# Attention and gated MLP on one core: other slots for the output projection's loads, four output tiles moved behind the last visit, other places for scores

## The chip, the cores and the metric

The kernel runs on one core of one Trainium2 chip. The metric is device time in microseconds (us) of one execution. Before the change three executions took 1666.72 to 1669.98 us, with a median of 1668.14 us. A separate, profiled execution took 1665.91 us; its profile spans 1664.1 us from the first to the last instruction.

## The reference

The input x is 2048 rows of 512 floats. All three parts of the result read its normalised rows.

```python
xn = _layernorm(x)
qkv = xn @ wqkv                      # 32 heads of 16
p = softmax(q k^T * 16**-0.5)        # 2048 x 2048 for each head
s = (p v, heads side by side) @ wo
r = relu(xn @ w1 + b1)               # 1792 wide
g = silu((r * r) @ w2 + b2)
out = x + s * g
```

## The kernel before, in words

**Precision.** Every product that must be exact to float32 is made of three matmuls on a high and a low part (high·high, high·low, low·high). A term list of such a product over four blocks of 128 rows has twelve matmuls.

**The loop.** After a lead (layer norm, q, k, v, written to DRAM), the attention runs in 512 *steps*. A *unit* is four heads times 512 queries; there are 32 units of 16 steps, and a step takes one block of 128 keys. For each step the kernel makes four scores on TensorE (`exp_mm`, L1255), four exponentials on ScalarE (L1261, into a `pt` tile), and four products with v (`pv_mm`, L375, called by `pv_step` two steps later). The maxima that the softmax subtracts are made a unit ahead by a second set of score matmuls (L300) and a reduction on VectorE (L308). The queue `SP` issues nearly all transfers, in program order.

**Lanes and visits.** A score has only 64 rows of contraction, so TensorE runs two at a time, one on array rows 0 to 63 and one on rows 64 to 127 (two *lanes*). The dense work (first the MLP, then the output projection) is cut into the same two lanes and mixed in by hand: `long_slots` handles four steps and one block of dense matmuls, a *visit* in two halves. At the end of a half stand the products with v of two earlier steps. When no maxima are left (`wide`), a half places ten pairs in a fixed order, a string in which `s` is a pair of scores and `D` a pair of dense matmuls. Places are counted from 0 here. In that stage the scores use five PSUM banks in turn, so a score can start only when the exponential five scores before it has been read.

**The output projection.** `wo_part` (L719) makes 14 visits from step 456 to step 511: the four tiles of output chunk 2, two of chunk 3, then the eight of chunks 0 and 1. Visit k starts at step 456 + 4k. Chunks 2 and 3 lack the last units, whose share is added later by `unit_out` (L844) with a small weight tile `w7`: for unit 30 four tiles of chunk 2 (`unit_inner`), for unit 31 the four tiles of chunk 3 (`unit_final`, after the last step). `wo_load(c)` brings the attention output of chunk c (three transfers of 512 KB, L685, for chunk 3 with a clearing on GpSimd first, L682; `wo_load_last` a fourth, L693), `wo_ask(k)` brings the gate g and, where needed, the rows of x for output tile k (L708, L713), and `wo_small` the small weight (cleared on GpSimd, L667, then loaded, `w7r`, L670). `fill` is a list of 24 matmuls for two tiles of chunk 3, kept to cover waits behind the last visit (L800).

**Due times.** `later(n, fn)` puts fn off: `begin(st)` at the start of each step runs what has come due, in the order in which it was put on the list. A call put off while such a list is being run can run at the next step at the earliest. The evacuation of a finished unit is a chain of such calls: the sums are taken out by a small transfer (`evac_sums`, L393), inverted on VectorE (`evac_recip`, L399), written and read back (L402, L407), multiplied in on GpSimd (L413 to L415) and stored (L422). VectorE works in program order, so a late sum holds everything behind the reciprocal.

Of the kernel before, what the change touches and what calls it, by code (L numbers as in the profile page):

```python
# [16 lines left out]
P = 128  # L17
S = 2048
D = 512
# [21 lines left out]
def kernel(  # L41
# [54 lines left out]
    with ExitStack() as ph:  # L96
# [84 lines left out]
        def later(n, fn):  # L181
            waiting.append((now[0] + n, fn))
# [470 lines left out]
            wos["w"] = wot  # L653

        def wo_pools():
            wos["f"] = right(wstk, "fp", 6)
            wos["oc"] = right(wstk, "ocp", 3)
            tail["p"] = right(wstk, "tailp", 1)
            free_pt.extend(
                tail["p"].tile([P, 512], F32, name=f"pt{NPT + i}") for i in range(4)  # L660
            )

        def wo_small():

            tp = tail["p"]
            raw = tp.tile([P, D], F32, name="w7r")
            nc.gpsimd.memset(raw, 0.0)  # L667
            for j in range(4):
                r = (H - 4 + j) * DH
                nc.sync.dma_start(raw[32 * j : 32 * j + DH, :], wo[r : r + DH, :])  # L670
            w7 = tail["w7"] = tp.tile([P, 2, D], F32R, name="w7")
            later(2, lambda: split((w7[:, 0], w7[:, 1]), raw))
            sel = tail["sel"] = tp.tile([P, 4], F32, name="sel")
            nc.gpsimd.tensor_scalar(
                sel, ident.rearrange("p (j r) -> p j r", r=32)[:, :, DH],
                1.0, 0.0, op0=ALU.mult, op1=ALU.add,
            )

        def wo_load(c):
            oc = wos["oc"].tile([P, 2, KO, 512], F32R, name="oc")  # L680
            if c == 3:
                nc.gpsimd.memset(oc[64:, :, 3].bitcast(F32), 0.0)  # L682
            for a, b in ((0, P), (P, 512)) if c == 2 else ((0, 512),):
                for ko in range(3):
                    nc.sync.dma_start(  # L685
                        oc[:, :, ko, a:b].bitcast(F32),
                        on_d[ko][:, :, c * 512 + a : c * 512 + b].rearrange("k p t -> p k t"),
                    )
            wos["oc", c] = oc

        def wo_load_last(c):
            n = P if c < 2 else 64
# [26 lines left out]
        def wo_part():  # L719
            for k in range(14):  # L720
                c, tt = WO_ORDER[k]
                if k == 0:
                    later(8, lambda: wo_load(3))
                    later(12, lambda: wo_load_last(3))
                if k == 4:
                    wo_load(0)
                if k == 6:
                    later(1, lambda: wo_load(1))
                if k == 5:
                    wo_load_last(0)  # L730
                if k == 9:
                    wo_load_last(1)
                if k < 12:
                    wo_ask(k + 2)
                if k == 11:
                    later(2, lambda: [wo_ask(14), wo_ask(15)])
                oc, wot = wos["oc", c], wos["w"]
                t0 = c * 512 + tt * P
                ts_ = slice(tt * P, (tt + 1) * P)
                g, xr = wos.pop(k)  # L740
                wide = c < 2 and m_free()
                if wide and "w" not in free_ps:
                    free_ps["w"] = [pm.tile([P, 512], F32, name="pm_t") for _ in range(3)]
                ps = [pd.tile([P, D], F32, name="pd_t")]
                ps.append(free_ps["w"][2] if wide else ps[0])
                if c > 1:
                    s = tail[c, tt] = tail["p"].tile([P, D], F32, name=f"ts{c}{tt}")

                def post():
                    if c > 1:  # L750
                        nc.scalar.activation(s, ps[0], AF.Copy)
                        nc.gpsimd.tensor_tensor(s, s, g, op=ALU.mult)
                        nc.gpsimd.tensor_tensor(s, s, xr, op=ALU.add)
                        return
                    if wide:
                        h = wos["f"].tile([P, D], F32, name="h", bufs=2)
                        nc.vector.tensor_tensor(h, ps[1], g, op=ALU.mult)
                        nc.gpsimd.tensor_tensor(xr, xr, h, op=ALU.add)
                    nc.vector.tensor_tensor(g, ps[0], g, op=ALU.mult)
                    nc.gpsimd.tensor_tensor(g, g, xr, op=ALU.add)  # L760
                    later(2, lambda g=g, t0=t0: nc.sync.dma_start(of[t0 : t0 + P, :], g))

                def emit(lane, n, i, m, kos):
                    r = slice(64 * lane, 64 * lane + 64)
                    a, b = ((0, 0), (0, 1), (1, 0))[i]
                    inst = nc.tensor.matmul(  # L766
                        ps[lane], oc[r, a, n, ts_], wot[r, b, n],
                        start=m == 0 and (lane == 0 or wide), stop=m == kos and (lane == 1 or wide),
                        skip_group_check=True,
                    )  # L770
                    if m == 0 and last_use[0] is not None and not wide:
                        tc.add_manual_dep(
                            inst.ins, last_use[0].ins.name,
                            mybir.DependencyInfo(
                                mybir.DependencyClass.Sync, mybir.DependencyReason.DATA
                            ),
                            reason="the other row tile is done with the bank",
                        )

                units = []  # L780
                for lane in range(2):
                    kos = [0, 1, 2] + [3] * (c < 2 or lane == 0)
                    terms = [(n, i) for n in kos for i in range(3)]
                    units.append([
                        lambda lane=lane, n=n, i=i, m=m, e=len(terms) - 1: emit(lane, n, i, m, e)
                        for m, (n, i) in enumerate(terms)
                    ])
                yield (units, post, 4) + ((True,) if wide else ())
# [55 lines left out]
        def unit_out(ps, c, tt, add, begun=False):  # L844
            hl, w7 = tail["hl"], tail["w7"]
            ts_ = slice(tt * P, (tt + 1) * P)
            for n, (i, k) in enumerate(((0, 0), (0, 1), (1, 0))):
                nc.tensor.matmul(
                    ps, hl[:, i, ts_], w7[:, k], start=(n == 0 and not begun), stop=(n == 2),
                    skip_group_check=begun,  # L850
                )
            k = 14 + 4 * (c - 2) + tt
            g, s = wos.pop(k)
            t0 = c * 512 + tt * P
            if k < 18:
                wo_ask(k + 2)
            if k == 17:
                later(1, lambda: [wo_ask(20), wo_ask(21)])
            nc.vector.tensor_tensor(g, ps, g, op=ALU.mult)
            add.tensor_tensor(g, g, s, op=ALU.add)  # L860
            if c == 2:
                later(1, lambda: nc.sync.dma_start(of[t0 : t0 + P, :], g))
            else:
                nc.sync.dma_start(of[t0 : t0 + P, :], g)

        def unit_inner(po):

            u = NU - 2
            ev = {"ot": sp.tile([P, 512], F32, name="ot", bufs=1)}
            nc.vector.tensor_scalar(ev["ot"], po, 1.0, 0.0, op0=ALU.mult, op1=ALU.add)  # L870
            for n, fn in zip(EVAC_LAST, (evac_sums, evac_recip, evac_keep, evac_back, evac_norm)):
                later(n, lambda fn=fn: fn(u, ev))

            def out(tt):
                tail["hl"] = ev["hl"]
                unit_out(pe.tile([P, 512], F32, name="se"), 2, tt, nc.gpsimd)

            for tt in range(4):
                later(9 + tt, lambda tt=tt: out(tt))

        def unit_final(po):
            ot = tail["ot"] = tail["p"].tile([P, 512], F32, name="tot")
# [2 lines left out]
            run_fill(2)  # L885
            unit_sums(pe, "se")
            run_fill(4)
            unit_norm(pe, "se", (nc.vector, nc.gpsimd))
            run_fill(len(fill))
            tail["ps", 0] = free_ps["w"][2]  # L890
            tail["ps", 1] = pd.tile([P, 512], F32, name="pd_t")
            for n, tt in enumerate((2, 3, 0, 1)):
                unit_out(
                    tail["ps", tt], 3, tt, nc.vector if n % 2 else nc.gpsimd, tt > 1
                )
# [438 lines left out]
        def long_slots(st0, units, post, wide=False):  # L1334
# [26 lines left out]
            for h in range(2):  # L1361
# [2 lines left out]
                    begin(st)  # L1364
                n = len(units[h])
                if wide:
                    for i, o in enumerate("sDDsDDsDsD"):
                        for lane in range(2):
                            if o == "s":
                                s(lane)  # L1370
# [87 lines left out]
        run_waiting(True)  # L1458
        assert not waiting and next(dn, None) is None
        fill_mms()  # L1460
        run_fill(13)
        for st_ in (NU * 16 - 2, NU * 16 - 1):
            pv_step(st_, pts.pop(st_))
        wstk.close()
# [26 lines left out]
```

## Time and profile before

| what | value |
|---|---|
| median of three executions | 1668.14 us |
| profiled execution | 1665.91 us |
| its span | 1664.1 us |
| TensorE (PE) busy | 1633.2 us, 98% |
| VectorE (DVE) busy | 1341.3 us, 81% |
| ScalarE (ACT) busy | 1185.3 us, 71% |
| GpSimd (POOL) busy | 511.2 us, 31% |
| mean granted TensorE clock | 0.998 |

PE is the matmul row and PEld the weight loads that overlap it. The times of a timeline row are its start and its length; a bracket at its end tells how long the engine sat idle before it and what ended that. `SPq` rows are issues of transfers. In the chain, each row is a piece of the work that ended last, with its start and its share.

### The profile page before, as it was taken

What the parts mean: (1) busy time and instruction counts of PE and PEld (TensorE: products, weight loads), DVE (VectorE), ACT (ScalarE), POOL (GpSimd) and SP (SyncE); (2) the same over time, 40 slices, a digit from 0 to 9 for tenths busy, and PEclk for the clock granted to TensorE, in tenths of its full rate; (3) what the DMA queues carried; (4) which work ended last, traced back from release to release, by engine and by line L of the source; (5) the groups of instructions that cost most, each with busy time, mean ns of one, the idle gap of its engine ahead of it and who ended that gap; (6) DMA issues with size and microseconds to landing.
All of it is one profiled execution on the core that took longest, in us unless ns stands there. A gap on an engine that the chain in (4) does not pass through costs nothing.

```text
span 1664.1 us, 35934 instructions
## 1 busy us (share of the span) xinstructions
PE 1633.2 (98%) x13674; PEld 981.0 (59%) x13674; DVE 1341.3 (81%) x2299; ACT 1185.3 (71%) x2344; POOL 511.2 (31%) x534
## 2 busy tenths in 40 slices
PE   6999999999999999999999999999999999999998
PEld 4898666556656665665565456555654565544454
DVE  6499888887887788877888888888888888888822
ACT  6221487778878887887787777777777777777783
POOL 4435567513312221231133113201321233113134
PEclk9999999999999999999999999999999999999999
DMA  8677555425332522352243324342332442135433
GB/s 283 164 229 252 176 172 163 128 70 162 90 93 80 155 75 80 100 139 73 78 122 106 84 71 140 93 106 80 114 95 73 106 133 64 47 115 165 136 101 123
DMA packets 152980, 201.22 MB, mean 121 GB/s; under 512 B 50856, under 2 KB 70824, under 8 KB 151272
## 3 DMA queue, kind: packets, MB, share of 16 engines
q1 hardware_dynamic: 152808, 198.93, 41.3%
q8 instruction: 108, 1.77, 0.4%
q14 instruction: 64, 0.52, 0.1%
HBM read 144.58 MB, written 53.99 MB: 119 GB/s over the span
## 4 chain that ended last, share of the span: by engine, by line
PE 93%; DVE 3%; DMA 2%; issue 1%; ACT 1%; POOL 0%; SPq 0%; DVEq 0%; POOLq 0%; ACTq 0%
PE po L375 29%; PE pd_t L234 16%; PE pm_t L300 16%; PE se L1255 15%; PE pd_t L202 6%; PE se L1013 3%; PE pd_t L766 2%; DVE mx L308 2%; PE se L964 2%; PE pd_t L1013 1%; PE po L1013 1%; DMA xc<-xn_d 1%; DMA sm<-ot 1%; PE pm_t L336 1%; DMA xt<-in_A_x_dram 0%
## 5 line engine op out<-in xcount | busy, mean ns | idle before, releaser
L308 DVE TENSOR_REDUCE mx<-pm_t 128x1 f32<-128x512 f32 x2048 | 1266.1, 683 | 224.8 <-PE pm_t L300 130.4
L1261 ACT ACTIVATE pt<-se 128x512 f32<-128x512 f32 x1750 | 926.7, 615 | 234.7 <-PE se L1255 150.2
L300 PE MATMUL pm_t<-ka,qm 64*128 64x512 f32 x2048 | 779.7, 416 | 6.1 <-DVE mx L308 5.2
L1255 PE MATMUL se<-qe,ka 64*128 64x512 f32 x2016 | 746.5, 416 | 0.0
L375 PE MATMUL po<-pt,v 128*32 128x512 f32 x3564 | 525.5, 603 | 0.0
L300 PEld LDWEIGHTS pm_t<-ka,qm 64*128 64x128 f32 x2048 | 359.2, 184 | 215.4 <-DVE mx L308 203.4
L1255 PEld LDWEIGHTS se<-qe,ka 64*128 64x128 f32 x2016 | 353.2, 184 | 113.9 <-ACT pt L1261 68.4
L234 PEld LDWEIGHTS pd_t<-xc,w1s 64*128 64x128 f32 x2352 | 295.8, 187 | 44.1 <-issue 41.9
L234 PE MATMUL pd_t<-xc,w1s 64*128 64x256 f32 x2352 | 320.5, 286 | 0.0
L234 PE MATMUL pd_t<-w2t,hT 64*128 64x512 f32 x936 | 252.6, 406 | 0.0
L375 PE MATMUL po<-ex,v 128*32 128x512 f32 x532 | 213.3, 602 | 0.0
L1261 ACT ACTIVATE ex<-se 128x512 f32<-128x512 f32 x266 | 159.4, 615 | 45.0 <-PE se L1255 22.8
L234 PEld LDWEIGHTS pd_t<-w2t,hT 64*128 64x128 f32 x936 | 160.3, 184 | 43.9 <-issue 35.2
L375 PEld LDWEIGHTS po<-pt,v 128*32 128x32 f32 x3564 | 89.4, 108 | 156.4 <-issue 139.2
L549 POOL TENSOR_TENSOR r<-r 128x512 f32<-128x512 f32 x49 | 50.9, 1040 | 316.6 <-ACT r L546 316.6
L413 POOL TENSOR_TENSOR ot<-ot,hl 128x512 f32<-128x512 f32 x31 | 39.8, 1283 | 230.0 <-DMA hl<-r_d 158.2
L568 POOL TENSOR_TENSOR u<-u,b_t 128x512 f32<-128x512 f32 x16 | 20.5, 1284 | 285.1 <-ACT u L567 229.0
L202 PE MATMUL pd_t<-w2t,hT 64*128 64x512 f32 x408 | 106.2, 392 | 0.9 <-POOL w2t L81 0.8
L202 PEld LDWEIGHTS pd_t<-w2t,hT 64*128 64x128 f32 x408 | 72.6, 184 | 10.6 <-POOL w2t L81 1.2
L766 PE MATMUL pd_t<-wot,oc 64*128 64x512 f32 x258 | 75.8, 410 | 0.0
L81 POOL TENSOR_TENSOR hT<-r,hT 128x512 fp32r<-128x512 f32 x56 | 72.3, 1291 | 4.7
L1013 PE MATMUL se<-xT,wr_t 64*128 64x512 f32 x312 | 66.2, 391 | 0.0
(132 smaller groups left out, 1206.4 us busy)
## 6 DMA issues: line engine op xcount, KB each, us to landing
w1s<-w_d SPq DMA_DIRECT2D x196, 256.0 KB
qm<-q_d SPq DMA_DIRECT2D x384, 32.0 KB
qe<-q_d SPq DMA_DIRECT2D x384, 32.0 KB
ka<-k_d SPq DMA_DIRECT2D x96, 128.0 KB
xn_d<-xT SPq DMA_DIRECT2D x8, 1024.0 KB
k_d<-hl SPq DMA_DIRECT2D x32, 256.0 KB
q_d<-hl SPq DMA_DIRECT2D x32, 256.0 KB
xc<-xn_d SPq DMA_DIRECT2D x16, 512.0 KB
```

Of the source, the lines that this page charges most:

```text
L81: (lo or nc.gpsimd).tensor_tensor(dst[1], raw, dst[0].bitcast(F32), op=ALU.subtract)
L202: mm = nc.tensor.matmul(out_, lh(r), rh(r), start=first_ and lane == 0, stop=last_ and lane == 1, skip_group_check=True,)
L234: mm = nc.tensor.matmul(out_, lh(r), rh(r), start=first_ and lane == 0, stop=last_ and lane == 1, skip_group_check=True,)
L300: nc.tensor.matmul(ps, qms[u][p][64 * j : 64 * j + 64, qb * P : (qb + 1) * P], kas[qd, p][64 * j : 64 * j + 64, kc * 512 : (kc + 1) * 512] ...
L308: return nc.vector.tensor_reduce(mxs[u][:, c, kc : kc + 1], ps, axis=AX.X, op=ALU.max)
L375: nc.tensor.matmul(po[32 * j : 32 * j + 32, :], vs[qd][:, (4 * kb + j) * VW : (4 * kb + j) * VW + 32], pts[j], start=(kb == 0), stop=(kb = ...
L413: nc.gpsimd.tensor_tensor(ot, ot, hl[:, 1].bitcast(F32), op=ALU.mult)
L549: nc.gpsimd.tensor_tensor(r, r, r, op=ALU.mult)
L766: inst = nc.tensor.matmul(ps[lane], oc[r, a, n, ts_], wot[r, b, n], start=m == 0 and (lane == 0 or wide), stop=m == kos and (lane == 1 or ...
L1013: inst = nc.tensor.matmul(out_, lh(r), rh(r), start=first_ and lane == 0, stop=last_ and lane == 1, skip_group_check=True,)
L1255: nc.tensor.matmul(se, kas[qd, j // 2][b : b + 64, kb * P : (kb + 1) * P], qes[u][j // 2][b : b + 64, :], start=True, stop=True,)
L1261: return nc.scalar.activation(pts[j], se, AF.Exp, scale=0.25)
```

## The change

The loads of the output projection are given other due times. `wo_load(3)` runs two steps after visit 0 begins instead of eight, and its three transfers are put off by 0, 1 and 2 steps (the first two come to the next step, 459, the third to 460). `wo_load(0)` and `wo_load(1)` move from steps 472 and 481 to 474 and 487 and are spread in the same way; the fourth transfer of chunk 0 moves from 476 to 478. The g loads for the last eight output tiles are asked one per step from visit 12 on; to hold them, g has eight buffers instead of six. To make room, the ring of `pt` tiles gets three extra tiles instead of four, and the raw small weight uses a buffer of another pool.

The four `unit_out` calls for unit 30 leave the steps 9 to 12 after that unit's end and stand behind the last visit: three, then eight of the 24 filling matmuls, the fourth, then five more. Their stores are issued at once.

In `unit_final` both halves of the low part are made on VectorE, and the tiles are taken in the order 0, 1, 2, 3 instead of 2, 3, 0, 1.

In `wide` halves the order of pairs becomes `sDsDDsDDDs`.

```diff
         def wo_pools():
-            wos["f"] = right(wstk, "fp", 6)
+            wos["f"] = right(wstk, "fp", 8)
...
-                tail["p"].tile([P, 512], F32, name=f"pt{NPT + i}") for i in range(4)
+                tail["p"].tile([P, 512], F32, name=f"pt{NPT + i}") for i in range(3)
...
-            raw = tp.tile([P, D], F32, name="w7r")
+            raw = wos["f"].tile([P, D], F32, name="h", bufs=2)
...
+            wos["oc", c] = oc
+
+            def part(ko, a, b):
+                nc.sync.dma_start(
+                    oc[:, :, ko, a:b].bitcast(F32),
+                    on_d[ko][:, :, c * 512 + a : c * 512 + b].rearrange("k p t -> p k t"),
+                )
+
             for a, b in ((0, P), (P, 512)) if c == 2 else ((0, 512),):
                 for ko in range(3):
-                    nc.sync.dma_start(
-                        oc[:, :, ko, a:b].bitcast(F32),
-                        on_d[ko][:, :, c * 512 + a : c * 512 + b].rearrange("k p t -> p k t"),
-                    )
-            wos["oc", c] = oc
+                    if c == 2:
+                        part(ko, a, b)
+                    else:
+                        later(ko, lambda ko=ko: part(ko, 0, 512))
...
                 if k == 0:
-                    later(8, lambda: wo_load(3))
+                    later(2, lambda: wo_load(3))
                     later(12, lambda: wo_load_last(3))
                 if k == 4:
-                    wo_load(0)
-                if k == 6:
-                    later(1, lambda: wo_load(1))
+                    later(2, lambda: wo_load(0))
                 if k == 5:
-                    wo_load_last(0)
+                    later(2, lambda: wo_load_last(0))
+                if k == 7:
+                    later(3, lambda: wo_load(1))
                 if k == 9:
                     wo_load_last(1)
-                if k < 12:
-                    wo_ask(k + 2)
-                if k == 11:
-                    later(2, lambda: [wo_ask(14), wo_ask(15)])
+                wo_ask(k + 2)
+                if k >= 12:
+                    later(1, lambda k=k: wo_ask(k + 4))
+                if k == 13:
+                    for n in range(18, 21):
+                        later(n - 16, lambda n=n: wo_ask(n))
...
-            if k < 18:
-                wo_ask(k + 2)
-            if k == 17:
-                later(1, lambda: [wo_ask(20), wo_ask(21)])
+            if k == 14:
+                wo_ask(21)
             nc.vector.tensor_tensor(g, ps, g, op=ALU.mult)
             add.tensor_tensor(g, g, s, op=ALU.add)
-            if c == 2:
-                later(1, lambda: nc.sync.dma_start(of[t0 : t0 + P, :], g))
-            else:
-                nc.sync.dma_start(of[t0 : t0 + P, :], g)
+            nc.sync.dma_start(of[t0 : t0 + P, :], g)
...
-            for tt in range(4):
-                later(9 + tt, lambda tt=tt: out(tt))
+            tail["out"] = out
...
-            unit_norm(pe, "se", (nc.vector, nc.gpsimd))
+            unit_norm(pe, "se", (nc.vector, nc.vector))
...
-            for n, tt in enumerate((2, 3, 0, 1)):
+            for n, tt in enumerate(range(4)):
...
                 if wide:
-                    for i, o in enumerate("sDDsDDsDsD"):
+                    for i, o in enumerate("sDsDDsDDDs"):
...
         fill_mms()
-        run_fill(13)
+        for tt in range(3):
+            tail["out"](tt)
+        run_fill(8)
+        tail["out"](3)
+        run_fill(5)
```

## The prediction

> **What bounds the kernel now.** I read the page first, then the chain of waits over the last 60 us, then the timeline of single stretches. The page says that TensorE sets the pace, so a change is worth what it takes from TensorE's order of work or from its waits.
>
> ```profile
> PE 1633.2 (98%) x13674; PEld 981.0 (59%) x13674; DVE 1341.3 (81%) x2299; ACT 1185.3 (71%) x2344; POOL 511.2 (31%) x534
> PE 93%; DVE 3%; DMA 2%; issue 1%; ACT 1%; POOL 0%; SPq 0%; DVEq 0%; POOLq 0%; ACTq 0%
> ```
>
> The chain over the wide visits shows how regular they are, and what the four output tiles (L848) do to them.
>
> ```profile
> 1607.26 0.43 PE pm_t L1255
> ...
> 1611.94 0.42 PE pm_t L1255
> ...
> 1621.28 0.43 PE se L1255
> ...
> 1625.96 1.13 PE se L848 x3
> 1627.09 0.42 PE se L1255
> ...
> 1633.86 0.43 PE pm_t L1255
> ...
> 1639.81 0.43 PE pm_t L1255
> ```
>
> An undisturbed half takes 1611.94 - 1607.26 = 4.68 us; over three of them, (1621.28 - 1607.26) / 3 = 4.67. The three halves from 1621.28 to 1639.81, with the output tiles among them, take 18.53 instead of 14.01 us.
>
> **Part 1, places of scores.** This is one wide half in the timeline: its first score, two dense matmuls, the first and third exponential, the weight load of the eighth score, the last dense matmul. The last row, a view of the dense line, counts the wide visits.
>
> ```profile
> 1627.02 0.49 PE L1255 MATMUL se<-qe,ka 64*128 64x512 f32 x1
> ...
> 1627.35 0.39 PE L766 MATMUL pd_t<-wot,oc 64*128 64x512 f32 x1
> ...
> 1627.55 0.60 ACT L1261 ACTIVATE pt<-se 128x512 f32<-128x512 f32 x1 [1.78 <-PE pm_t L1255]
> 1627.58 0.39 PE L766 MATMUL pd_t<-wot,oc 64*128 64x512 f32 x1
> ...
> 1628.52 0.61 ACT L1261 ACTIVATE pt<-se 128x512 f32<-128x512 f32 x1
> ...
> 1629.18 0.18 PEld L1255 LDWEIGHTS se<-qe,ka 64*128 64x128 f32 x1 [0.25 <-ACT pt L1261]
> ...
> 1629.52 0.38 PE L766 MATMUL pm_t<-wot,oc 64*128 64x512 f32 x1
> ...
> L766 PE MATMUL pm_t<-wot,oc x60: 383/390/397, 1593.5 to 1642.3; 64*128 64x512 f32 x60
> ```
>
> Place 1 begins 0.33 us after place 0, each later one 0.23 after its neighbour, so place i is due at 0.33 + 0.23 (i - 1): place 8 at 1.94, place 9 at 2.17. The eighth score (place 8) needs the bank of the third. That exponential ends at 1628.52 + 0.61 = 1629.13, 2.11 into the half; the score starts 0.05 later, 2.16, and holds the dense matmul behind it on its lane: 2.50 instead of about 2.19. Each wide half loses 0.31.
>
> With the new string the scores stand at places 0, 2, 5 and 9. The sixth (place 5, due at 1.25) needs the first exponential, 1.13 + 0.05 = 1.18; the eighth (place 9, due at 2.17) needs 2.16. Both just fit, so a half shrinks to about 4.36. ScalarE keeps up: starts (1628.52 - 1627.55) / 2 = 0.49 apart make eight exponentials 3.9 us. Sixty matmuls at twelve a visit are five wide visits, ten halves: -3.1 us. It cannot cost: both waiting scores stand for exponentials that the old order waited for too. The bounds are 0 (place 5 stands instead) and -3.1; I take the full sum, since the rows leave it room.
>
> The ring of pt tiles, one shorter, costs nothing: a wide half needs sixteen, and the second exponential of a half, the first to take a tile that the products just freed, starts a microsecond after them. If that cover went, the exponential would wait for the end of the products, some tenths each half.
>
> **Part 2, the four output tiles.** In the loop they cost 18.53 - 14.01 = 4.52 us: twelve matmuls, and waits before and behind them. Behind the last visit they stand with the filling matmuls, of the same form, whose pace the timeline shows:
>
> ```profile
> 1644.47 3.28 PE L800 MATMUL pm_t<-wot,oc 128*128 128x512 f32 x13
> ...
> 1647.69 1.92 PE L375 MATMUL po<-pt,v 128*32 128x512 f32 x16
> ```
>
> 3.22 / 13 = 0.248 each; twelve take 2.97. The banks they want are those of the last scores, whose exponentials are over 0.53 + 7 x 0.49 + 0.6 = 4.6 us into the half, 0.2 behind its end, and the fourth tile stands behind eight fills so that VectorE has read the first one's bank. GpSimd's four additions (1.26 us each, the L860 row of part 3) end before the final tiles want it, and the stores are out long before the end. Net -1.55 us; bounds 0 (at 1.13 / 3 = 0.38 a matmul, as in the first loop tile) and -1.8 (at the 0.23 of a wide half's places). The asks for g move by a few steps and land at least one half before their use: nothing. If one were late, VectorE would wait there, under the fills.
>
> **Part 3, the last unit.** The end of the profile, with the high parts, the low parts, the first product's reading, and the last additions:
>
> ```profile
> 1653.65 0.75 ACT L838 ACTIVATE thl<-tot 128x256 fp32r<-128x256 f32 x2 [3.58 <-DVE tot L837]
> 1654.10 0.43 DVE L840 TENSOR_TENSOR thl<-tot,thl 128x256 fp32r<-128x256 f32 x1
> 1654.47 0.73 POOL L840 TENSOR_TENSOR thl<-tot,thl 128x256 fp32r<-128x256 f32 x1 [8.32 <-ACT thl L838]
> 1655.79 0.69 DVE L859 TENSOR_TENSOR g<-pm_t,g 128x512 f32<-128x512 f32 x1 [1.27 <-PE pm_t L848]
> ...
> 1659.09 1.26 POOL L860 TENSOR_TENSOR g<-g,ts 128x512 f32<-128x512 f32 x1 [1.23 <-DVE g L859]
> 1659.64 1.25 DVE L860 TENSOR_TENSOR g<-g,ts 128x512 f32<-128x512 f32 x1
> ```
>
> Now tile 2 comes first and waits for the low part on GpSimd (1655.20). In the new order tile 0 wants only the first low part (1654.53), so its product can be read at about 1655.1, 0.7 earlier; the second low part on VectorE is done by 1655.0. On that clock VectorE then reads tiles 0 and 1 to 1656.5, adds tile 1, reads 2 and 3, adds tile 3. The last addition above, started under GpSimd's (until 1660.35), ends 0.54 behind it. If each of VectorE's additions ends so, 0.54 behind GpSimd's, the last ends at 1660.3 instead of 1660.89: -0.6. Without that wait the same steps end 1.2 us sooner still. [...] Bounds -0.2 (tile 0 waits for both low parts) and -0.9.
>
> **Part 4, the loads.** The one long stop of the loop is here:
>
> ```profile
> 1497.49 1.27 POOL L752 TENSOR_TENSOR ts<-ts,g 128x512 f32<-128x512 f32 x1
> 1500.07 0.54 POOL L667 MEMSET w7r<- 128x512 f32 x1
> 1500.63 1.74 SPq L670 DMA_DIRECT2D w7r<-in_A_wo_dram  x4
> 1507.48 2.72 SPq L132 DMA_DIRECT2D qe<-q_d  x6
> 1509.59 0.95 POOL L682 MEMSET oc<- 64x1024 f32 x1
> 1510.25 1.45 SPq L685 DMA_DIRECT2D oc<-on_d  x3
> 1512.80 4.50 SPq L132 DMA_DIRECT2D qe<-q_d  x6
> 1517.67 3.82 SPq L132 DMA_DIRECT2D qm<-q_d  x6
> 1521.59 0.62 SPq L393 DMA_DIRECT2D sm<-ot  x1
> 1523.56 0.25 DVE L399 RECIPROCAL sm<-sm 128x16 f32<-128x16 f32 x1 [2.85 <-DMA sm<-ot]
> 1524.41 0.61 PE L300 MATMUL pm_t<-ka,qm 64*128 64x512 f32 x1 [2.36 <-DVE mx L308]
> 1525.00:1530.00 5.00, 5.00 (x32) 1.62 (x28) 3.07 (x6) 2.09 (x4) 0.00 (x0) 0.69 0.58 175
> SPq L132 <- DMA oc<-on_d: 2.0, 2, 1.1
> ```
>
> SP issues the sums of unit 28 at 1521.59; they land 1.97 later; VectorE has stood 2.85 at the reciprocal, and TensorE 2.36 behind it. Right after, the window from 1525 to 1530 has a granted clock of 0.69: 0.31 x 5 = 1.55 more. The stop costs 3.9 us. [...]
>
> SP is late since 1500.63, where it had waited for the clearing of w7r; from there it issues without rest. Between w7r and the sums it issues 37 transfers: 4 for w7r, 4 shift rows, 4 g and x, 4 stores, 12 qe, 6 qm and 3 oc. In the new order all 37 still stand between them. At step 459 the list holds w7r, then the shift rows, then the first two oc loads; 460 has the third. They move ahead of other transfers, not ahead of w7r. The two held groups take (4.50 - 2.72) + (3.82 - 2.72) = 2.9 us more than a free six; the last row has the cause, issues that wait for an oc load which brings them no data (the eighth command ahead: as if eight may be under way). The same 1.5 MB will hold the stores and the first qe in their stead, as long. The new clearing of oc (0.95), due at 458, stands ahead of both L752 and the clearing of w7r, so SP starts up to 0.95 later. Between 0 and 0.95 I take the middle: sums at 1522.1, +0.5 us. The stop stays. Bounds: -3.9 (no hold at all: sums 2.9 us sooner, when VectorE comes to them) and +2 (the whole delay and a hold longer by a microsecond).
>
> The other two loads have room on SP:
>
> ```profile
> 1555.89 2.65 SPq L132 DMA_DIRECT2D qe<-q_d  x6
> 1583.67 0.34 SPq L761 DMA_DIRECT2D out_dram<-g  x1
> ```
>
> SP waits for other engines ahead of each of these rows, some microseconds long. Chunk 0 now fits the pause before the first, chunk 1 the one before the second, and that is 9.8 us before the first wide visit (1593.5); the shift rows and stores standing behind them have as long. They cost nothing; a load late for its visit would stop TensorE for as long as it is late.
>
> **Sum.** -3.1 - 1.55 - 0.6 + 0.5 = -4.75 us: span 1659.3, profiled execution 1661.2. The profiled execution before is 2.2 us under the median of the runs; applied to that, 1668.14 - 4.75 = 1663.4 us.
>
> **Rivals.** *The stop goes too* (15%): the spread loads hold SP no more, and the reciprocal finds its sums. For it: the hold is 2.9 us, and 2.85 are wanted. Against: the unchanged count of issues and the clearing. 1663.4 - 0.5 - 3.9 = 1659.0.
>
> *The new places gain nothing* (14%): the sixth score at place 5 has 0.07 us of room, the eighth 0.01; if the first exponential comes later by 0.3, the half is as long as before. For it: such small room. Against: ScalarE has 4.36 - 3.9 us to spare in a half, so its first exponential follows the first score at once. 1663.4 + 3.1 = 1666.5, no measurable difference.
>
> *Slower* (10%): the stop grows. The three oc loads stand ahead of stores and qe, and SP is held longer than my count; each microsecond that the sums come later is one of TensorE, and a pause reaching into another 3.4 us window adds 1.55. For it: SP has no slack there and starts later. Against: the bytes are the same. To undo 4.75 takes 3.2 us of stop and one window; to be 0.2% slower takes 8.05 us, so sums 6.5 later than I forecast, at 1528.6. At that point the time is 1671.4.
>
> **Chances.** My forecast has 61%; its own range, from the bounds of the parts, is 1661.5 to 1665.7. With the stop gone at one end and the lost places at the other, each with the bounds of the other parts, the range is 1657.8 to 1667.4. About 0.2%, 3.3 us, is what a measurement can tell from no change. Faster: most of my case and the first rival, 0.72; same: the second and an edge of mine, 0.18; slower 0.10.
>
> **What would show it.** Wide halves 4.36 us apart, with no wait for ScalarE at the eighth score; no L848 before the last visit's end, and about 6.2 us between its products and the last ones; tile 0 first at the end; the sums of unit 28 still issued near 1522, with VectorE idle before L399 and a clock dip. A filled stop, or halves of 4.67, would make the forecast wrong.

## The result, and the profile after

| | before | after |
|---|---|---|
| median of 17 executions each | 1667.99 us | 1664.39 us |
| lowest and highest | 1665.85 and 1670.05 | 1660.91 and 1667.35 |
| profiled execution | 1665.91 us | 1665.93 us |
| its span | 1664.1 us | 1664.2 us |

The ratio is 0.9982, with a 95% interval of 0.9974 to 0.9989: the change takes off 3.6 us, 1.8 to 4.3 by the interval. The forecast was 4.75 us less and a median of 1663.4.

The two profiled executions are equally long, so they have to be read by stretches. The products with v of one step are a good ruler; "product n" below is the start of those of step n, as the timeline gives it. First the kernel before, then the one after, at products 430, 462, 470 and 510: the first stands ahead of everything that the change touches.

```profile
1420.07 1.07 PE L375 MATMUL po<-pt,v 128*32 128x512 f32 x8
...
1511.60 1.06 PE L375 MATMUL po<-pt,v 128*32 128x512 f32 x8
...
1538.41 1.07 PE L375 MATMUL po<-pt,v 128*32 128x512 f32 x8
```

```profile
1421.93 1.07 PE L375 MATMUL po<-pt,v 128*32 128x512 f32 x8
...
1514.05 1.06 PE L375 MATMUL po<-pt,v 128*32 128x512 f32 x8
...
1543.30 1.06 PE L375 MATMUL po<-pt,v 128*32 128x512 f32 x8
...
1648.43 1.93 PE L375 MATMUL po<-pt,v 128*32 128x512 f32 x16
```

At product 430 the profiled execution after is already 1421.93 - 1420.07 = 1.86 us late, through nothing that was changed (the last section shows where). From there to the end it takes 1.8 us less (242.2 against 244.0). The stretch with the stop, 462 to 470, takes 29.25 instead of 26.81 us: it alone gives back 2.44. Another 0.64 us go at the start of the output projection (4.19 us from product 453 to 454, 3.55 before), where TensorE waits for a load of the attention output (0.19 us of idle time ahead of the dense matmul at 1490.65); e2 below, with the same loads, does not have that (3.54), so it is not the change's doing. What the change gained lies behind product 470.

**The wide halves and the output tiles.** The chain of the kernel after (start, length, what):

```profile
1606.97 0.43 PE se L1258
...
1638.08 0.43 PE pm_t L1258
...
1642.53 2.27 PE se L857 x9
1644.79 1.85 PE pm_t L809 x8
1646.65 0.69 PE se L857 x3
```

Seven halves take 1638.08 - 1606.97 = 31.11 us, 4.444 each (4.67 before, 4.36 forecast). No output tile (L857, L848 before) interrupts them; the twelve matmuls behind the visit take 2.27 + 0.69 = 2.96 us.

**The end.** The timeline after has both low parts on VectorE (L849, x2); its last additions (L867) are:

```profile
1654.84 0.76 DVE L849 TENSOR_TENSOR thl<-tot,thl 128x256 fp32r<-128x256 f32 x2 [0.15 <-ACT thl L847]
...
1659.15 1.26 POOL L867 TENSOR_TENSOR g<-g,xr 128x512 f32<-128x512 f32 x1 [1.23 <-DVE g L866]
1659.71 1.26 DVE L867 TENSOR_TENSOR g<-g,xr 128x512 f32<-128x512 f32 x1
```

The last addition ends at 1660.97, 12.54 us after product 510; before it was 1660.89 - 1647.69 = 13.20. That is 0.66 less, and the whole tail behind product 510 goes from 16.40 to 15.72.

**The stop.** The timeline, two windows (length, busy time of PE, PEld, DVE, ACT and POOL, granted clock, DMA share, GB/s), and two rows of the queue's waits:

```profile
1499.88 0.95 POOL L682 MEMSET oc<- 64x1024 f32 x1
1503.49 0.53 POOL L667 MEMSET h<- 128x512 f32 x1
1504.05 1.74 SPq L670 DMA_DIRECT2D h<-in_A_wo_dram  x4
1513.35 4.94 SPq L132 DMA_DIRECT2D qe<-q_d  x6
1525.78 0.62 SPq L393 DMA_DIRECT2D sm<-ot  x1
1527.75 0.25 DVE L399 RECIPROCAL sm<-sm 128x16 f32<-128x16 f32 x1 [4.59 <-DMA sm<-ot]
1528.60 0.79 PE L300 MATMUL pm_t<-ka,qm 64*128 64x512 f32 x1 [4.11 <-DVE mx L308]
1525.00:1530.00 5.00, 1.40 (x6) 1.16 (x8) 2.25 (x5) 0.31 (x2) 0.00 (x0) 0.68 0.26 63
1530.00:1535.00 5.00, 5.00 (x28) 1.43 (x24) 2.64 (x5) 2.08 (x5) 0.00 (x0) 0.64 0.55 161
SPq L670 <- POOL sel L674: 8.1, 1, 8.1
SPq L132 <- DMA oc<-on_d: 2.8, 2, 2.0
```

The wait of 8.1 us stands at the root. Its row names `sel` (L674), which GpSimd starts just as the clearing of h ends (1503.49 + 0.53 = 1504.02); the issue follows at 1504.05. The small weight (now tile h, L670) starts 10.00 us before product 462, where it was 10.97: 0.97 later, the new clearing of oc (0.95) ahead of it on GpSimd. From it to the sums SP needs 21.73 us instead of 20.96. So the sums are issued 1.74 us later, 11.73 behind product 462, and TensorE stands 4.11 instead of 2.36 us.

The clock is lost for longer too. The two windows have 0.32 x 5 and 0.36 x 5 us less of it, which is 6.8 us at half speed, from 1526.8 on. But the pause lasts from 1524.49 to 1528.60, so TensorE still stands in the first 1.8 us of that. The rest costs (6.8 - 1.8) / 2 = 2.5 us, against 1.7 before, where one stretch of 3.4 us at half speed (1524.65 to 1528.06) began as the pause had ended (1524.41). That is 0.8 more, and with the 1.75 of the longer pause 2.55, near the 2.44 by which the stretch grew.

### The profile page after: what moved, and what is told of

The parts are those of the page before. It is cut to its first block, busy times and chain, and to the rows that moved or that the text cites. A ratio compares the mean times of both kernels' runs of the same rounds, so it can differ in the third digit from the quotient of the medians.

```text
span 1664.2 us, 35916 instructions
## 1 busy us (share of the span) xinstructions
PE 1630.7 (98%) x13674; PEld 983.9 (59%) x13674; DVE 1342.1 (81%) x2300; ACT 1185.6 (71%) x2344; POOL 511.3 (31%) x533
## 4 chain that ended last, share of the span: by engine, by line
PE 92%; DVE 3%; DMA 2%; SPq 1%; ACT 1%; issue 0%; POOL 0%; DVEq 0%; ACTq 0%; POOLq 0%
PE po L375 29%; PE pd_t L234 16%; PE pm_t L300 16%; PE se L1258 15%; PE pd_t L202 5%; PE se L1016 3%; DVE mx L308 2%; PE pd_t L775 2%; PE se L967 2%; PE pd_t L1016 1%; PE po L1016 1%; DMA sm<-ot 1%; SPq L132 1%; PE pm_t L336 1%; DMA wv<-in_A_wqkv_dram 0%; DMA oc<-on_d 0%
## 5 line engine op out<-in xcount | busy, mean ns | idle before, releaser
L202 PEld LDWEIGHTS pd_t<-w2t,hT 64*128 64x128 f32 x408 | 73.1, 185 | 11.8 <-POOL w2t L80 1.6
```

The costliest lines, as they stand in the source:

```text
L202: mm = nc.tensor.matmul(out_, lh(r), rh(r), start=first_ and lane == 0, stop=last_ and lane == 1, skip_group_check=True,)
```

## The experiments

All medians are beside runs of the kernel before on the same chip. "462 to 470" is the stretch with the stop, "430 to end" the part that the change can touch, both read from the profiled execution by the starts of the products. The kernel after has 17 executions, e1 to e3 and e5 to e7 have 8 to 11, the others 5.

| kernel | median us | ratio to before, 95% | 462 to 470 | 430 to end |
|---|---|---|---|---|
| before | 1667.99 | | 26.81 | 244.0 |
| after | 1664.39 | 0.9982 (0.9974 to 0.9989) | 29.25 | 242.2 |
| e1_old_loads | 1663.33 | 0.9970 (0.9958 to 0.9981) | 26.76 | 239.1 |
| e2_old_order | 1667.39 | 0.9993 (0.9984 to 1.0002) | 29.31 | 244.0 |
| e3_old_last_unit | 1664.94 | 0.9985 (0.9974 to 0.9996) | 27.99 | 242.0 |
| e4_early_w7r | 1657.47 | 0.9939 (0.9927 to 0.9951) | 22.61 | 235.1 |
| e5_before_early_w7r | 1665.27 | 0.9987 (0.9978 to 0.9995) | 23.71 | 241.1 |
| e6_out_in_loop | 1667.81 | 1.0000 (0.9991 to 1.0009) | 29.49 | 244.9 |
| e7_clear_behind | 1663.93 | 0.9977 (0.9967 to 0.9986) | 27.52 | 240.2 |
| e8_early_w7r_old_loads | 1658.70 | 0.9954 (0.9941 to 0.9968) | 23.47 | 236.0 |
| e9_sums28_act | 1660.09 | 0.9950 (0.9937 to 0.9962) | 23.86 | 237.1 |
| e10_early_w7r_sums_act | 1676.39 | 1.0051 (1.0037 to 1.0065) | 23.28 | 238.5 |

The theory was that of the prediction: three parts gain, and the loads do not take the stop away, since SP is late from the small weight on. The rivals were that the stop's cause lies elsewhere (the burst of oc loads), and that one of the three parts does nothing.

**e1_old_loads**: the kernel after with the loads at their old places.

```diff
-                    if c == 2:
-                        part(ko, a, b)
-                    else:
-                        later(ko, lambda ko=ko: part(ko, 0, 512))
+                    part(ko, a, b)
...
-                    later(2, lambda: wo_load(3))
+                    later(8, lambda: wo_load(3))
...
-                    later(2, lambda: wo_load(0))
+                    wo_load(0)
...
-                    later(2, lambda: wo_load_last(0))
-                if k == 7:
-                    later(3, lambda: wo_load(1))
+                    wo_load_last(0)
+                if k == 6:
+                    later(1, lambda: wo_load(1))
```

> The changed kernel with the loads of chunks 3, 0 and 1 at their old steps, three in a burst; all else as changed. Theory (the new due times hold SP longer in front of the sums of unit 28, so the stop near 1522 grew from 2.36 to 4.09 us of idle TensorE and from one half-clock window to two): sums some 1.7 us sooner against the products around them, idle back at about 2.4 us, one window at most, and the time 1.7 to 3.4 us under the changed kernel's 1664.4, so 1661.0 to 1662.7, about 6 us under the kernel before. Rival (the longer stop was an accident of the one profiled execution): no difference from the changed kernel, 1664.4, 3.6 us under the kernel before.

The stretch is back at 26.76, so its growth belongs to the loads. The other kernels below that keep the new loads and the late small weight, e2, e3 and e6, have 29.31, 27.99 and 29.49. Parts 1 to 3 alone are 1663.33 - 1668.03 = -4.70 us against the runs of before beside it. The loads cost 2.5 us in the profiled pair and 1.06 in the medians, whose intervals overlap.

**e2_old_order**: the old string.

```diff
-                    for i, o in enumerate("sDsDDsDDDs"):
+                    for i, o in enumerate("sDDsDDsDsD"):
```

> The changed kernel with the old places of scores in wide halves; all else as changed. Theory (each of ten halves shrank from 4.67 to 4.45 us): halves of 4.67 again and 2.2 us more than the changed kernel, about 1666.6, 1.4 us under the kernel before. Rival (the halves shrank because the output tiles left the loop, not by the order): halves stay near 4.45 and the time stays at 1664.4.

Its chain shows the old length again with nothing in between, (1643.78 - 1606.39) / 8 = 4.674:

```profile
1606.39 1.85 PE po L375 x16
...
1643.78 1.85 PE po L375 x16
```

From product 490 to 510 it takes 49.89 us, the kernel after 47.82: 2.07 for nine halves. The median is 3.0 us above that of the kernel after, so the string is worth 2 to 3 us. Against before (51.70) the same stretch gives the four output tiles under the old string: 1.81.

**e6_out_in_loop**: the four output tiles back in the steps 9 to 12 behind unit 30, with the old asks and stores.

```diff
...
-            tail["out"] = out
+            for tt in range(4):
+                later(9 + tt, lambda tt=tt: out(tt))
...
-        for tt in range(3):
-            tail["out"](tt)
-        run_fill(8)
-        tail["out"](3)
-        run_fill(5)
+        run_fill(13)
```

This is a part of the edit; the asks for g and the stores go back in the same way.

> The changed kernel with the four output tiles of unit 30 in the loop again, with their old asks and stores, and 13 fills behind the last visit; all else as changed. Theory (in the loop they cost 4.5 us, behind it 3.0 to 3.4): 1.1 to 1.5 us more than the changed kernel, 1665.5 to 1665.9. Rival (with the new places of scores their waits in the loop are gone too): halves with output tiles only 3 x 0.25 longer, nothing lost, 1664.4.

The products before and behind the half with the first three matmuls, and a pause between them:

```profile
1626.18 1.93 PE L375 MATMUL po<-pt,v 128*32 128x512 f32 x16
...
1629.45 0.50 PE L855 MATMUL se<-w,hl 128*128 128x512 f32 x1 [0.62 <-POOL hl L415]
...
1633.91 1.92 PE L375 MATMUL po<-pt,v 128*32 128x512 f32 x16
```

This half takes 7.73 us instead of 4.44 (the longest of before, with a tile in it, 7.02). The stretch 490 to 510 is 50.75, so the move is worth 2.93 us under the new string (3.4 by the medians) and 1.81 under the old one: with the new places a tile in the loop stalls more. TensorE's pauses at these tiles are 0.62 us for the last GpSimd step of the unit's evacuation, and twice 0.48 for an exponential, where the kernel before has two of 0.25. The two edits are worth more together than the sum of each alone, and the 3.4 us are over twice what was expected before the run.

**e3_old_last_unit**: the second low part on GpSimd, and the old order of the last tiles.

```diff
-            unit_norm(pe, "se", (nc.vector, nc.vector))
+            unit_norm(pe, "se", (nc.vector, nc.gpsimd))
...
-            for n, tt in enumerate(range(4)):
+            for n, tt in enumerate((2, 3, 0, 1)):
```

> The changed kernel with the last unit's second low part on GpSimd and its tiles in the order 2, 3, 0, 1 again. Theory: the stretch from the last products with v to the end, 0.64 us shorter after the change, gets those 0.64 back: 1665.0. Rival (the end is set by the last store alone): the stretch stays as it is in the changed kernel, 1664.4.

```profile
1648.47 1.92 PE L375 MATMUL po<-pt,v 128*32 128x512 f32 x16
...
1655.25 0.74 POOL L849 TENSOR_TENSOR thl<-tot,thl 128x256 fp32r<-128x256 f32 x1 [5.78 <-ACT thl L847]
...
1660.42 1.26 DVE L867 TENSOR_TENSOR g<-g,ts 128x512 f32<-128x512 f32 x1
```

The last addition ends at 1661.68, 13.21 behind product 510, as before the change: 0.67 is this part's. The medians (0.55) cannot show it by themselves.

**e4_early_w7r and e5_before_early_w7r**: the cause of the stop. The small weight is loaded where it is first due, three steps earlier, in the kernel after (e4) and in the kernel before (e5).

```diff
-            later(3, wo_small)
+            wo_small()
```

> The changed kernel with the small weight cleared and loaded three steps earlier, at step 456, so that SP does not stand 8 us for GpSimd at the clearing and then work off 37 issues in a row. Theory (that wait is the root of the stop in both kernels): SP reaches the sums of unit 28 before VectorE reaches the reciprocal, no idle TensorE and no half clock there; 4.1 us of idle and up to 3.4 us of clock go: 1657 to 1660, 8 to 11 us under the kernel before. Rival (SP is held by eight transfers under way, whatever stands at its head): the sums come at most 2 us sooner, the stop stays at 2 us or more, and the time is no better than 1662.

> The kernel before with one edit: the small weight is cleared and loaded at step 456 instead of 459. Theory (the wait for GpSimd at its clearing is the root of the stop already before the change): the sums of unit 28 come some 5 us sooner, no idle TensorE and no half-clock window near 1522; the 4.2 us of that stop go, 1663.8. Rival (the old burst of three loads at step 464, late in front of the sums, is the root): the stop keeps 2 us or more, 1666 to 1668.

The small weight, the sums and their use in e4, in the timeline:

```profile
1491.30 1.81 SPq L670 DMA_DIRECT2D h<-in_A_wo_dram  x4
...
1518.64 0.62 SPq L393 DMA_DIRECT2D sm<-ot  x1
...
1523.30 0.24 DVE L399 RECIPROCAL sm<-sm 128x16 f32<-128x16 f32 x1
```

The sums leave 4.35 us behind product 462 (1514.29), and the reciprocal has no idle time in front of it. The stretch is 22.61 us, without pause or lost clock (granted clock 1.00 from 1505 to 1535): the stop had cost 29.25 - 22.61 = 6.64 us, and the median falls by 6.9. This kernel beats the kernels before and after, with intervals apart. In e5 the stop shrinks, but does not go:

```profile
1517.04 4.36 SPq L132 DMA_DIRECT2D qe<-q_d  x6
1521.77 3.56 SPq L132 DMA_DIRECT2D qm<-q_d  x6
1525.43 0.62 SPq L393 DMA_DIRECT2D sm<-ot  x1
1527.40 0.25 DVE L399 RECIPROCAL sm<-sm 128x16 f32<-128x16 f32 x1 [1.21 <-DMA sm<-ot]
```

There the three oc loads in a burst still hold the qe and qm issues in front of the sums, and the reciprocal waits 1.21 us.

**e8_early_w7r_old_loads**: e4 with the old loads of e1, so that the four kernels of loads and small weight are complete.

> The changed kernel with the small weight at step 456 and with the loads of chunks 3, 0 and 1 at their old steps in bursts. Theory (once SP is not late, it does not matter where these loads stand): no stop, 1657.5 like the changed kernel with the early small weight alone. Rival (the spread loads are needed as well): a stop of 1 us or more comes back, 1659 to 1662.

```profile
1521.40 0.25 DVE L399 RECIPROCAL sm<-sm 128x16 f32<-128x16 f32 x1 [0.94 <-DMA sm<-ot]
```

| median us (462 to 470) | small weight late | small weight early |
|---|---|---|
| loads in bursts | 1663.33 (26.76) | 1658.70 (23.47) |
| loads spread | 1664.39 (29.25) | 1657.47 (22.61) |

Spreading the loads lengthens the stretch by 2.5 us where SP is late from the small weight on, and shortens it by 0.86 where it is not, each read from one profiled execution. The medians have the same signs, but in neither row of the comparison do their intervals part.

**e7_clear_behind**: the clearing of oc two steps later, behind that of the small weight on GpSimd.

```diff
-                nc.gpsimd.memset(oc[64:, :, 3].bitcast(F32), 0.0)
+                later(2, lambda: nc.gpsimd.memset(oc[64:, :, 3].bitcast(F32), 0.0))
```

> The changed kernel with the clearing of the loaded chunk put off by two steps, so that on GpSimd it stands behind the clearing of the small weight; the loads themselves as changed. Theory (of the 1.74 us that the sums came later, 0.95 are this clearing, the rest a longer hold of SP by the loads): sums 0.8 us later than before the change against the products around them, idle TensorE near 3.2 us, 1 us under the changed kernel's time, 1663.4. Rival (the hold alone): sums as late as in the changed kernel, 1664.4.

```profile
1503.78 2.13 SPq L670 DMA_DIRECT2D h<-in_A_wo_dram  x4
1525.48 0.62 SPq L393 DMA_DIRECT2D sm<-ot  x1
```

With product 462 at 1514.80, the small weight starts 11.02 us before it (before: 10.97) and the sums leave 10.68 behind it. Of the 1.74 us of delay 1.05 go with the clearing; 0.69 stay, the longer hold. The medians do not tell it from the kernel after.

**e9_sums28_act**: only the sums of unit 28 leave on ScalarE's queue.

```diff
-            nc.sync.dma_start(
+            (nc.scalar if u == 28 else nc.sync).dma_start(
```

> The changed kernel with one edit: the sums of unit 28 alone are issued from ScalarE's queue instead of SP's; SP's order and lateness stay. Theory (the stop is only that this one small transfer stands behind SP's late issues): the reciprocal finds its sums, no idle TensorE near 1525, no half-clock window there; products 462 to 470 take 22.6 to 23 us instead of 29.2; the time is that of the early small weight, 1657.5 to 1659. Rival (other transfers of the late queue, the qm loads above all, would stop TensorE next): a stop of a microsecond or more moves to a maximum that waits for qm, 1660 to 1663.

```profile
1517.64 1.11 ACTq L393 DMA_DIRECT2D sm<-ot  x1
1519.45 0.50 PE L1258 MATMUL se<-qe,ka 64*128 64x512 f32 x1 [0.89 <-ACT pt L1264]
```

One transfer on another queue, and the reciprocal has no idle time in front of it, although SP's own list is as late as ever: the stop was TensorE's wait for the late issue of the sums, and for nothing else in that list. The price is on ScalarE: its issue takes 1.11 us, and TensorE then waits 0.89 for an exponential. The median is 8.8 us under that of the kernel before beside it; that of e4 is 10.6 under.

**e10_early_w7r_sums_act**: e4, and the sums of all units on ScalarE's queue.

```diff
-            nc.sync.dma_start(
+            nc.scalar.dma_start(
```

> The changed kernel with the small weight at step 456 and the sums of all units issued from ScalarE's queue. Theory (in the MLP stage too VectorE stands 0.7 to 2.2 us at some reciprocals behind SP's queue, near 251, 929 and 1298): those waits go, 1 to 2 us less than with the early small weight alone, 1655.5 to 1656.5; the half-clock window near 298, which follows waits for GpSimd, stays. Rival (the issue takes ScalarE's time at every unit end, or those waits had no price): 1657.5 or more.

The issues, from the groups, and TensorE's waits for ScalarE over the whole span:

```profile
L393 ACTq DMA_DIRECT2D sm<-ot x31: 529/546/1111, 241.6 to 1620.8; - x31
```

```profile
PE se L1258 <- ACT pt L1264: 11.8, 30, 2.0
```

This kernel is the slowest, 18.9 us above e4. Thirty times, about once a unit, the scores wait for an exponential that stands behind the issue, 11.8 us in all; the same view of e4 has no such row. The stretch from product 66 to 430 grows from 1029.4 to 1041.2 us. Of these 11.8 us the waits explain 7.4: 22 of the thirty lie in that stretch. The 22 issues in it take 12.0 us of ScalarE together, which is near the growth, but no run separates the issue from the waits behind it. Another 3.4 lie behind product 430 (238.5 against 235.1); what remains of the medians' difference is not traced.

## Why the prediction was right, and where it was not

The prediction was right in sign and about right in size: 3.6 us less where it had 4.75. By its own parts:

**Part 1, -3.1 forecast, -2.26 measured** (ten halves by 4.67 - 4.444). The mis-sized term is the half of 4.36 us. The places were right, and so was the forecast that both waiting scores nearly fit. What it left out is in these rows of the timeline after, a half that starts at 1620.24:

```profile
1620.24 0.50 PE L1258 MATMUL se<-qe,ka 64*128 64x512 f32 x2
...
1621.75 0.60 ACT L1264 ACTIVATE pt<-pm_t 128x512 f32<-128x512 f32 x1
...
1622.21 0.18 PEld L1258 LDWEIGHTS se<-qe,ka 64*128 64x128 f32 x1
...
1622.40 0.18 PEld L1258 LDWEIGHTS pm_t<-qe,ka 64*128 64x128 f32 x1
1622.46 0.43 PE L1258 MATMUL pm_t<-qe,ka 64*128 64x512 f32 x1
...
1622.83 1.93 PE L375 MATMUL po<-pt,v 128*32 128x512 f32 x16
```

The third exponential ends at 1622.35, 2.11 into the half, as forecast. But it is the weight load of the eighth score that stands for it: it starts at 1622.40, where its neighbour's went at 1622.21, and the score follows at 1622.46, 2.22 into the half instead of 2.17. Then the products begin at 2.59 instead of 2.51. The room of 0.01 us that the prediction counted at place 9 was for the score, not for its weights. No run took this wait away, so the last 0.08 us are read from rows, not tested.

**Part 2, -1.55 forecast, -1.81 measured** under the old string (e2 against before), at the bound of -1.8. The 2.97 behind the visit came out at 2.96; what the move frees in the loop is larger than the 4.52 forecast. That the string and the tiles act on each other (2.93 under the new string, e6) is not in the sum.

**Part 3, -0.6 forecast, -0.67 measured.** The forecast that VectorE's additions end 0.54 behind GpSimd's held: the last pair ends at 1660.41 and 1660.97, 0.56 apart. So the gain is the smaller one and not the 0.6 + 1.2 = 1.8 us of the author's estimate without that wait. What makes VectorE's addition end so far behind GpSimd's, no run shows.

**Part 4, +0.5 forecast, +1.1 by the medians of e1, +2.5 in the profiled pair.** The mechanism was right: the stop stays, the 37 issues stay between, the new clearing delays the small weight. Two terms were mis-sized. "Between 0 and 0.95 I take the middle" should have been the whole: the clearing stands ahead on GpSimd and nothing covers it (0.97). And "as long" was wrong for the hold: from the small weight to the sums SP needs 0.77 more (0.74 in e7, without the clearing in front), and its waits for oc loads grew from 2.0 to 2.8 us (two each; by the order of the queue's rows each of the four waiting issues is the eighth behind an oc load). Why the spread loads hold it longer is not shown. Together the sums are 1.74 us later, and the pause reaches into a second window of lost clock, the step that the prediction had only in its slower rival. The 3.4 us window of that rival is measured, the stretch at half speed of before; its 1.55 for one more was the author's estimate from the clock of 0.69, and here the second window cost 0.8, since TensorE stood in the first 1.8 us of the two. By the profiled pair that is past the bound of +2. The other two loads cost nothing, as forecast: from product 470 to 490 the kernel after takes 57.31 us, before it was 57.58. And the stop of before, put at 3.9 us, is worth 26.81 - 22.61 = 4.2, if e4 is what remains without it.

The measured parts give -2.26 - 1.81 - 0.67 = -4.74 without the loads, against -4.70 in the medians of e1, whose interval is wider than this agreement (3.2 to 7.0 us less). The forecast for these three was -5.25: what part 1 lacks, parts 2 and 3 make up in part, and that is luck. With the loads it is -3.6 by the medians. By the profiled execution it is -4.74 + 2.44 + 0.64 = -1.7 behind product 430, where -1.8 were read. The forecast's own range, 1661.5 to 1665.7, is not the sum of the parts' bounds: with the new places kept and the stop still there these give 1662.3 to 1666.8. The measured 1664.39 lies in both.

**The rivals.** *The stop goes too*: not here, but e4 shows it was within one line: not the spread of the loads, but the small weight decides. *The new places gain nothing*: no, 2 to 3 us. *Slower because the stop grows*: it did grow by the mechanism named, with the sums 1.2 us later than forecast, of the 6.5 that would have made the kernel slower.

## What to carry to other kernels

Where one queue issues in program order, look for the first row where it waits long for another engine, and count what is queued behind it: here a wait of 8.1 us for a clearing was followed by 37 issues ahead of a small transfer, and loading the small weight three steps earlier was worth more (6.9 us) than the whole change (3.6). In these profiled executions spreading the loads helped only once the queue was not late already; while it was, what came ahead of the critical issue was paid at TensorE. On ScalarE's queue, which TensorE waits for, nearly every issue was paid in e10 (30 waits, 11.8 us, behind 31 of them), so move the one transfer that is late and not all.

## What the runs showed of the hardware

**Short pauses lose the clock, and not in every execution.** Early in the loop, at the same place, TensorE waits for GpSimd's splitting of a weight. First a window of the kernel before with its pause, then the same of e4 and of the kernel after:

```profile
295.00:300.00 5.00, 4.12 (x30) 1.97 (x29) 3.51 (x7) 2.92 (x6) 3.26 (x4) 1.00 0.51 156
297.13 0.50 PE L202 MATMUL pd_t<-w2t,hT 64*128 64x512 f32 x1 [0.85 <-POOL w2t L81]
```

```profile
296.26 0.50 PE L202 MATMUL pd_t<-w2t,hT 64*128 64x512 f32 x1 [0.94 <-POOL w2t L80]
297.62 0.50 PE L202 MATMUL pd_t<-w2t,hT 64*128 64x512 f32 x1 [0.85 <-POOL w2t L81]
295.00:300.00 5.00, 3.21 (x20) 0.72 (x16) 2.33 (x5) 1.91 (x4) 3.11 (x4) 0.86 0.54 151
```

```profile
295.91 0.50 PE L202 MATMUL pd_t<-w2t,hT 64*128 64x512 f32 x1 [1.18 <-POOL w2t L80]
297.26 0.50 PE L202 MATMUL pd_t<-w2t,hT 64*128 64x512 f32 x1 [0.85 <-POOL w2t L81]
295.00:300.00 5.00, 3.23 (x16) 0.90 (x18) 1.73 (x4) 1.32 (x3) 4.24 (x5) 0.80 0.60 161
```

In the kernel before one pause of 0.85 us leaves the clock at 1.00; in e4 two of 0.94 and 0.85 us, 1.4 us apart, do not (0.86), and in the kernel after two of 1.18 and 0.85 us do not (0.80). In e10 two waits for the same splitting, 0.9 and 0.7 us, keep it: its mean granted clock is 1.000 over the whole execution. The kernels do the same work there. Before product 430 the profiled execution before has no such dip and the one after has this one; e8 and e9 have none, with a mean clock of 1.000 like that of e10. Between products 2 and 66, where this lies, the profiled execution after takes 190.57 us and that of before 188.11: more than the 1.86 us by which it is late at product 430, and the reason why two profiled executions of equal length hide a gain.

**In these traces what counts is how long TensorE stands inside one window.** In the traces of before and after, the half-speed stretches ahead of the last products are 3.41 us long (from 1524.65 before, from 297.97 after) or 6.83 (from 1526.77 after). With the ones at the very end (from 1661.18 and 1659.89) they start on one grid of 3.41 us in each execution: 40 of its steps apart before, 360 and 39 after. Each follows a window of that grid in which TensorE's matmul rows leave 1.83 us or more idle. From 25 us on, no window of the two traces with 1.15 us or less idle was followed by half speed, and none had between 1.15 and 1.83. So the pauses of 1.18 and 0.85 us in the kernel after lie in one window (294.56 to 297.97) and count together, 2.03 us. At its stop the boundary at 1526.77 cuts the pause of 4.11 into 2.28 and 1.83 us, and two windows are lost; in e3, with a pause of 3.44 us, the matmul rows are longer (0.53 to 0.79 us, against 0.39) only from 1529.76 to 1533.7, and one is lost. The boundaries lie at other places of the work in each execution: the first behind product 462 comes 2.81 us after it in before and 2.48 us after it in after.

**A pause that grows can cost more than its length.** From 2.36 to 4.11 us of pause (1.75 more) the stretch grew by 2.44, with the second window. In e3 and e7, which have the same loads or nearly, pauses of 3.44 and 3.06 us met one window (in e7 clocks of 0.84 and 0.82 over 1525 to 1535, 3.4 us at half speed) and the stretch grew by 1.2 and 0.7 only, about as much as the pause did. The kernel after and e3 run the same program up to there; so which of the two a given execution gets is not settled by the program, and the cost of the new loads has no single value.
